# Moving early key transposes, summing early sketches in PSUM, moving the clears of later rows, and joining the last stores in a sketch-attention and top-2 expert kernel

## The chip, the cores and the metric

The kernel runs on one core of a Trainium2 chip. The metric is the device time in microseconds (us) of one execution; lower is better. The engines are TensorE (PE; PEld is its weight load), VectorE (DVE), ScalarE (ACT), GpSimd (POOL) and SyncE (SP). SP, ACT and POOL issue the DMA transfers here, and POOL also the indirect ones, which scatter rows to addresses held in a tile.

## The reference, cut to what matters

Everything is float32. Batch 4, 4 heads of 32 dimensions, 1088 tokens: 4352 tokens of width 128 in all. Eight experts with an inner width of 1024.

```python
def phi(x):                       # r = 8
    a = einsum('rd,bhsd->bhsr', S1, x)
    b = einsum('rd,bhsd->bhsr', S2, x)
    return einsum('bhsi,bhsj->bhsij', a, b).reshape(..., 64)
q_p, k_p = phi(q), phi(k)
kv  = einsum('bhsf,bhsd->bhfd', k_p, v)
z   = sum(k_p, axis=2)
x   = (q_p @ kv) / (q_p . z + 1e-6)          # per head, then heads side by side: 128 wide
logits = x @ w_gate
noisy  = logits + log1p(exp(x @ w_noise)) * noise
top2   = the two largest of noisy per token; weights = their softmax
out    = sum over the token's two experts of weight * (relu(x @ w1[e]) @ w2[e])
```

## The kernel before

**Order.** Nothing is issued in the order in which the program text stands. `plan.add` records a job with its engine or engines, an estimated cost, what it reads and writes, and a priority; `Plan.order` simulates the engines with these costs and, among the jobs that could start soonest, takes the one with the lowest priority number. Each engine and each queue then executes its jobs in that fixed order, so a job that waits holds up everything behind it on its engine. `idle` (line 1435 is its matmul) fills the planner's gaps on PE before 28 us with bf16 matmuls on a zero tile, `hp<-zb`, whose results nobody uses.

**The head (batch 0).** `sk` (L541) is the sketch matrix, split into a main part and a correction, `sk[:, 0]` and `sk[:, 1]`, 64 columns each. `turned` (L588, L590) transposes keys or queries on DVE into `kT` or `qT`. `features` multiplies up to four token tiles by all 128 columns of `sk` (L606) into one PSUM bank, copies the correction's half to `lo` (L322 is the copy helper), adds it to the main half into `ab` (L614) and forms the 64 products per head (`product`, L628) in `phk` or `phq`. `vaug` is the values with a column of ones, copied by ACT or POOL. L669 sums keys times values; two ACT copies make `kvT`; `fold` (L690) multiplies it by the gate weights; two copies make `kvw`, left and right columns of one tile. `queries` turns `phq` on PE (L717), copies it to `pT`, and L728 gives numerators, denominators and gate logits at once; `den` (L757) and `lg` (L747) follow on DVE.

**Routing.** `router` chooses the two experts of a tile's tokens and writes each weighted token row with its number to its expert's area in `xs`, one indirect scatter of 128 rows at a time (`xs<-xg,to`, L809; L808 is a short memset on POOL ahead of each as a spacer). One call of `router` is a wave; wave 0 is the first four tiles of batch 0, wave 1 the other five. Before a wave's rows are scattered, the rows it may reach must have been cleared: `clear` writes a pad tile of zeros over 128 rows of all experts, 516 KB each, issued by SP. Dependencies on `paces` put each scatter behind a chosen step of ACT or DVE.

**Expert blocks.** A block is one unit u: 128 or 256 rows of an expert. The first `DIRECT` = 4 units don't read `xs`: one-hots `o` on DVE (L1054), every fourth on ACT (L1047, L1050), gather the tokens by a matmul (`turn`, L1060). Units 4 to 7 are fetched by POOL and turned on PE (L1084); from 8 on SP fetches four pieces and DVE transposes them (L1096). `bT` is a unit's rows, transposed. L1108 multiplies them by `w1`, L1116 is the relu, L1123 multiplies by `w2` into `acc`; `y` is its copy, which POOL scatters to the token's place in `pairs`. For the first four units those places are in `first_at`, for the others in `ix`, fetched by SP.

**The end.** `sums` loads `pr` from `pairs`, adds a token's two results (L1179) and stores them. For the last batch the last two experts' results don't go through `pairs`: `to_tokens` adds them by one-hot matmuls (L1255) into `totals`, and `more` (L1186) adds those before the store, which ACT issues. There are three pieces: tiles 4 and 5, the 64 rows left over, tiles 6 and 7.

## Time and profile before

| | us |
|---|---|
| runs: median, lowest, highest | 346.61, 346.3, 347.8 |
| profiled execution, its own time | 347.08 |
| its span, from the first to the last instruction | 345.1 |
| busy: PE, POOL, DVE, ACT | 336.2, 232.1, 146.4, 136.4 |
| granted TensorE clock, mean over the span | 0.994 |
| first and second expert matmul of all blocks (L1108, L1123) | 147.3, 149.8 |

The rows of a timeline give the start, the length, the engine, the line, the operation, the tiles as output<-inputs and the count; consecutive instructions of one kind are drawn together. What stands in brackets is how long the engine had been idle and what ended that. A matmul in float32 appears as two records. A DMA row shows the issue on its queue, not the transfer.

### The profile page before, as it was taken

The page shows a single profiled execution, that of the slowest core. Times are in us where ns is not written, and L with a number is a line of the kernel's source. Part 1 is how long each engine was busy: PE and PEld are TensorE (multiplying, and loading weights), DVE is VectorE, ACT ScalarE, POOL GpSimd, SP SyncE. Part 2 cuts the span into 40 slices and gives each one's busy share as a digit, 9 for nine tenths or more (in the row PEclk, how much of TensorE's full clock was granted, in tenths as well). Part 3 has the DMA queues.
Part 4 walks back from the last instruction along what each step waited for, and adds up shares of the span by engine and source line. Part 5 has one row for each costly group of instructions (what it writes and reads, how often), then busy time and mean ns, then how long its engine had stood idle before and what let it go on. Part 6 is the DMA issues. An engine that isn't in the chain of part 4 may idle for free.

```text
span 345.1 us, 7493 instructions
## 1 busy us (share of the span) xinstructions
PE 336.2 (97%) x2585; PEld 313.9 (91%) x2586; DVE 146.4 (42%) x547; ACT 136.4 (40%) x305; POOL 232.1 (67%) x385
## 2 busy tenths in 40 slices
PE   8999999999999999999999999999999999999992
PEld 3859999999999999999999999999999999999992
DVE  5889794877636688555862000020102000112101
ACT  2357542543531445323334333433334333434430
POOL 8854868896899857898968889878334433354410
PEclk9999999999999999999999999999999999999997
DMA  7999839144571376511353213365125211114421
GB/s 217 327 346 268 288 63 356 60 116 114 139 221 39 62 187 133 138 40 39 74 74 71 54 43 54 69 184 120 37 36 185 67 32 27 29 32 166 147 77 39
DMA packets 68922, 41.17 MB, mean 119 GB/s; under 512 B 49877, under 2 KB 61078, under 8 KB 68880
## 3 DMA queue, kind: packets, MB, share of 16 engines
q1 hardware_dynamic: 63360, 30.93, 35.1%
q0 software_dynamic: 4704, 9.15, 8.2%
q10 hardware_dynamic: 816, 0.58, 0.6%
q8 instruction: 21, 0.34, 0.4%
q14 instruction: 21, 0.17, 0.2%
HBM read 24.18 MB, written 16.65 MB: 118 GB/s over the span
## 4 chain that ended last, share of the span: by engine, by line
PE 95%; DVE 2%; ACT 1%; issue 1%; POOL 0%; DVEq 0%; ACTq 0%; POOLq 0%
PE acc L1123 37%; PE hp L1108 37%; PE bank L606 5%; PE bank L728 4%; PE bank L669 4%; PE bank L717 2%; PE hp L1435 1%; PE acc L669 1%; PE bank L1255 1%; PE turn L1060 1%; PE bank L690 0%; ACT o L1050 0%; PE bank L937 0%; DVE lg L747 0%; ACT o L1047 0%
## 5 line engine op out<-in xcount | busy, mean ns | idle before, releaser
L1123 PEld LDWEIGHTS acc<-w2s,h 128*128 128x128 f32 x1152 | 145.8, 192 | 4.6
L1123 PE MATMUL acc<-w2s,h 128*128 128x128 f32 x1152 | 149.8, 275 | 0.0
L1108 PE MATMUL hp<-bT,w1s 128*128 128x128 f32 (+1 forms) x768 | 147.3, 328 | 0.2 <-ACT bT L322 0.2
L1116 ACT ACTIVATE h<-hp 128x512 f32<-128x512 f32 x144 | 86.0, 597 | 123.2 <-PE hp L1108 122.9
L1108 PEld LDWEIGHTS hp<-bT,w1s 128*128 128x128 f32 x768 | 111.6, 191 | 6.4 <-ACT h L1116 0.5
L809 POOL DMA_INDIRECT pairs<-y,ix x66 | 65.1, 986 | 66.1 <-ACT y L322 55.9
L809 POOL DMA_INDIRECT xs<-xg,to x72 | 73.0, 1014 | 19.2 <-issue 9.1
L808 POOL MEMSET zb<- 128x400 bf16 (+1 forms) x142 | 63.1, 444 | 0.2 <-PE hp L1435 0.2
L1096 DVE STREAM_TRANSPOSE bT<-xb 128x256 f32<-128x256 f32 (+1 forms) x40 | 15.6, 390 | 101.9 <-PE hp L1108 89.8
L322 ACT COPY y<-acc 128x128 f32<-128x128 f32 (+1 forms) x48 | 15.3, 320 | 28.1 <-PE acc L1123 27.6
L1179 DVE TENSOR_TENSOR o<-pr 128x512 f32<-128x512 f32 (+2 forms) x13 | 6.7, 525 | 36.1 <-DMA pr<-pairs 36.1
L728 PE MATMUL bank<-kvw,pT 128*128 128x98 f32 x144 | 18.2, 274 | 0.0
L728 PEld LDWEIGHTS bank<-kvw,pT 128*128 128x128 f32 x144 | 17.4, 192 | 0.6 <-DVE kvw L322 0.3
L669 PE MATMUL bank<-phk,vaug 128*128 128x128 f32 (+1 forms) x108 | 13.1, 277 | 0.0
L322 ACT COPY lo<-bank 128x256 f32<-128x256 f32 (+3 forms) x20 | 6.5, 328 | 16.5 <-PE bank L606 16.5
L322 ACT COPY pT<-bank 128x512 f32<-128x512 f32 (+1 forms) x16 | 8.8, 559 | 10.6 <-PE bank L717 9.1
L669 PEld LDWEIGHTS bank<-phk,vaug 128*128 128x128 f32 (+1 forms) x108 | 12.5, 191 | 0.4
L614 DVE TENSOR_TENSOR ab<-bank,lo 128x256 f32<-128x256 f32 (+3 forms) x20 | 7.2, 360 | 12.5 <-ACT lo L322 12.4
L628 DVE TENSOR_TENSOR phk<-ab 128x512 f32<-128x512 f32 (+1 forms) x20 | 12.2, 629 | 0.4
L628 DVE TENSOR_TENSOR phq<-ab 128x512 f32<-128x512 f32 (+1 forms) x20 | 11.8, 628 | 0.2
L991 DVE TENSOR_TENSOR xg<-x,g 128x512 f32<-128x512 f32 (+1 forms) x16 | 11.2, 750 | 0.0
L1435 PE MATMUL hp<-zb 128*128 128x512 bf16 x29 | 9.5, 463 | 1.6 <-DVE zb L439 1.3
(177 smaller groups left out, 243.7 us busy)
## 6 DMA issues: line engine op xcount, KB each, us to landing
xs<-pad SPq DMA_DIRECT2D x9, 516.0 KB
w1s<-in_moe_w_dram SPq DMA_DIRECT2D x8, 512.0 KB
w2s<-in_moe_w_dram SPq DMA_DIRECT2D x8, 512.0 KB
pr<-pairs SPq DMA_DIRECT2D x7, 512.0 KB
xb<-xs SPq DMA_DIRECT2D x96, 32.0 KB
kq<-in_k_dram SPq DMA_DIRECT2D x4, 544.0 KB
kq<-in_q_dram SPq DMA_DIRECT2D x4, 544.0 KB
vld<-in_v_dram SPq DMA_DIRECT2D x14, 128.0 KB
```

Of the source, the lines that this page charges most:

```text
L322: paces.append(A.copy(o, i) if e == "ACT" else V.tensor_copy(o, i))
L606: T.matmul(ps.t[rows, 2 * W * i:2 * W * i + 2 * W], lhsT=lhsT, rhs=sk[:].rearrange("p c h x -> p (c h x)"), start=True, stop=True)
L628: V.tensor_tensor(out=jobs[i][2].t[rows, jobs[i][1]:jobs[m - 1][1] + 1, :, :].rearrange("p c h (i j) -> p (c h) i j", i=R), in0=factors(i, ...
L669: T.matmul(kvp.t[:, P * a:P * a + P], lhsT=va.t[0:K, t, hs, :].rearrange("p h d -> p (h d)"), rhs=pk.t[0:K, t, hs, :].rearrange("p h f -> ...
L728: T.matmul(ps2.t[:, c0:c0 + 2 * YW], lhsT=pT.t[:, P * (2 * i + a):P * (2 * i + a) + P], rhs=kvw.t[:, a, :], start=True, stop=True)
L808: G.memset(zb[:, 0:FIRST_SPACER if kind == "first" else SPACER], 0.0)
L809: ins = G.indirect_dma_start(**kw)
L1096: add("DVE", vec(P * n), lambda _: V.transpose(bT.t[:, 0:P * n], flat()), r=[xb], w=[bT], prio=TOP + u)
L1108: T.matmul(hp.t[:, P * n * i:P * n * (i + 1)], lhsT=w1s[:, e, P * (js * g + i):P * (js * g + i + 1)], rhs=bT.t[:, 0:P * n], start=True, st ...
L1116: paces.append(A.activation(out=h.t[:], in_=hp.t[:], func=AF.Relu))
L1123: T.matmul(acc.t[:, D * c:D * c + D], lhsT=h.t[:, P * (n * i + c):P * (n * i + c + 1)], rhs=w2s[:, e, j, :], start=(j == 0 and c == 0), st ...
L1435: ins = T.matmul(warm()[:], lhsT=zb[:, 0:P], rhs=zb[:], start=True, stop=True)
```

## The change

- In the head, the first two tiles of keys are transposed before `sk` is made, and the other key transposes follow at once; `lo` is gone: the copy goes to `ab` and the add works in place.
- The early sketches, four tiles of queries of batch 0 and four of keys of batch 1, are each made by two matmuls of 64 columns that add up in PSUM, and ACT copies the result to `ab`.
- The two copies to `kvw` are one on ACT, one on DVE, and declared independent. The transposes of batch 1's keys follow them.
- On POOL the pad, the limits and the token numbers go behind the `vaug` copies, the limits in pieces, the last of them behind the first wave's choice of rows.
- The first unit's fourth one-hot is made by DVE as the others are.
- The clears of rows 256 to 511 go behind SP's four `ix` fetches; the planner treats two POOL jobs as behind the units' fetches. In the order that results, the clears of rows 0 to 255 stand behind the weights of expert 2 on SP, and POOL scatters the results of units 0 and 1 before the ten scatters of wave 1 (before: unit 0's alone).
- At the end the 64 rows come first and tiles 4 to 7 are read in two transfers and stored in one, two ACT issues for three. Tiles 0 to 3 of that batch are now read in two transfers too.

```diff
...
             for d in j.deps:
-                if d.engine == e and d.size is None and not d.far:
+                if d.engine == e and (d.size is None and not d.far or d in j.issued):
                     at = max(at, d.end)
...
     tag("qT", 1, [P, S])
-    tag("lo", 2, [P, 4, 2 * R * H])
-    tag("ab", 2, [P, 4 * H, 2, R])
+    tag("ab", 4, [P, 4 * H, 2, R])
     tag("kvT", 2, [P, 2, R * R])
...
-        add("POOL", cost, lambda e: emit(), r=r, w=w, prio=prio)
+        job = add("POOL", cost, lambda e: emit(), r=r, w=w, prio=prio)
+        if 11 < prio < 11.5:
+            behind_values.append(job)
+        if prio == 17:
+            behind_choices.append(job)
+
+    behind_values, behind_choices = [], []
...
-        pool_job(1.2, 13, pads, ["pad"])
+        pool_job(1.2, 11.45, pads, ["pad"])
...
-        pool_job(0.5, 14, lambda: limits(0, 1), [("limits", 0)], ["base"])
+        pool_job(0.5, 11.47, lambda: limits(0, 1), [("limits", 0)], ["base"])
...
                                channel_multiplier=2 * TN)
-        pool_job(2.4, 15, numbers, ["pid"])
-        pool_job(3.0, 16, lambda: limits(1, NW + 1), [("limits", 1)], ["base"])
+        pool_job(2.4, 11.4, numbers, ["pid"])
+        for w in range(1, NW + 1):
+            pool_job(0.5 if w < NW else 0.3, 16 if w < 4 else 17, lambda w=w: limits(w, w + 1), [("limits", 1)], ["base"])
         add("DVE", 0.3, lambda e: (V.tensor_copy(starts[:, 0, :], base[:]), V.memset(over[:], -1.0)),
...
-    def features(jobs, prio, after=(), first=None, early=None):
+    def features(jobs, prio, after=(), first=None, early=None, summed=False):
...
+                if summed:
+                    for c in range(2):
+                        T.matmul(ps.t[rows, W * i:W * i + W], lhsT=lhsT, rhs=sk[:, c, :, :].rearrange("p h x -> p (h x)"),
+                                 start=(c == 0), stop=(c == 1))
+                    continue
...
-        last = (add if early is None else plan.add)("PE", n * mm(128), emit, lat=0.15, r=["sk"] + [(xT, t) for xT, t, _ in jobs],
+        last = (add if early is None else plan.add)("PE", n * (2 * mm(64) if summed else mm(128)), emit, lat=0.15, r=["sk"] + [(xT, t) for xT, t, _ in jobs],
...
-        lo, ab = new("lo"), new("ab")
-        gone = [] if early is None else [onehot["pos"], onehot["gm"]]
+        ab = new("ab")
+        flat = lambda: ab.t[rows, 0:n * H, :, :].rearrange("p (i h) w r -> p i (h w r)", h=H)
...
-        add(EV, either(W * n), lambda e: copy(e, lo.t[rows, 0:n, :], x4()[:, :, 1, :]), r=[ps] + gone, w=[lo], prio=prio)
-        add("DVE", vec(W * n), lambda e: V.tensor_tensor(
-            out=ab.t[rows, 0:n * H, :, :].rearrange("p (i h) w r -> p i (h w r)", h=H),
-            in0=x4()[:, :, 0, :], in1=lo.t[rows, 0:n, :], op=ALU.add), r=[ps, lo], w=[ab], prio=prio if early is None else 12.95 if jobs[0][2] is kv_of[0][1] else 13.2)
+        if summed:
+            add("ACT", act(W * n), lambda e: copy(e, ab.t[rows, 0:n * H, :, :].rearrange("p x w r -> p (x w r)"), ps.t[rows, 0:W * n]),
+                r=[ps], w=[ab], prio=prio if early is None else 12, after=() if early is None else (onehot["sp"],))
+        else:
+            add(EV, either(W * n), lambda e: copy(e, flat(), x4()[:, :, 1, :]), r=[ps], w=[ab], prio=prio)
+            add("DVE", vec(W * n), lambda e: V.tensor_tensor(out=flat(), in0=x4()[:, :, 0, :], in1=flat(), op=ALU.add), r=[ps], w=[ab],
+                prio=prio)
...
-    behind_gates = []
+    behind_gates, folded_first = [], []
...
-            add(("ACT", "POOL") if head else "ACT", {"ACT": act(256), "POOL": 0.4} if head else act(256), lambda e, h=h: copy(e, va.t[:, 0:C, h, 0:DH], vld.t[:, h, 0:C, :]),
-                r=["ones_v"] + [(vld, l) for l in range(4)], w=[(va, h)], prio=prio + 2.2, after=hold)
+            value = add(("ACT", "POOL") if head else "ACT", {"ACT": act(256), "POOL": 0.45} if head else act(256),
+                        lambda e, h=h: copy(e, va.t[:, 0:C, h, 0:DH], vld.t[:, h, 0:C, :]),
+                        r=["ones_v"] + [(vld, l) for l in range(4)], w=[(va, h)], prio=prio + (2.05 if head else 2.2), after=hold)
+            if head:
+                for job in behind_values:
+                    job.deps.add(value)
...
-                turned(kT, kld, c0, c1, 22, True)
-                features([(kT, t, pk) for t in range(c0, c1)], prio + i + 1, after, 21.5, early)
+                turned(kT, kld, c0, c1, 22, True).deps.update(folded_first)
+                features([(kT, t, pk) for t in range(c0, c1)], prio + i + 1, after, 21.5, early, True)
...
-            freed.append(turned(kT, kld, c0, c1, prio + i))
+            freed.append(turned(kT, kld, c0, c1, (-51, 0.5, 0.9)[i] if head else prio + i))
...
-        freed.append(turned(kT, kld, 8, 9, prio + 1))
+        freed.append(turned(kT, kld, 8, 9, prio + (1.9 if head else 1)))
...
-            add(EV, either(98), lambda e, l=l: copy(
-                e, kvw.t[64 * l:64 * l + 64, :, YW * l:YW * l + YW],
-                ps.t[64 * l:64 * l + 64, 0:2 * YW].rearrange("p (a y) -> p a y", a=2)),
-                r=[ps, "kvw0"], w=[(kvw, l)], prio=prio + 3)
+            def half(e, l=l):
+                ins = copy(e, kvw.t[64 * l:64 * l + 64, :, YW * l:YW * l + YW],
+                           ps.t[64 * l:64 * l + 64, 0:2 * YW].rearrange("p (a y) -> p a y", a=2))
+                if head:
+                    apart(ins, "kvw")
+                    wrote(ins, "kvw")
+            done = add(("ACT", "DVE")[l] if head else EV, 0.25 if head else either(98), half, r=[ps, "kvw0"], w=[(kvw, l)], prio=prio + 3)
+            if head:
+                folded_first.append(done)
...
-                features([(qT, t, pq) for t in range(4, 8)], prio + 26, (), prio + 11, early)
+                features([(qT, t, pq) for t in range(4, 8)], prio + 26, (), prio + 11, early, True)
...
         actf(0.25, lambda: A.activation(out=t3("u"), in_=t3("u"), func=AF.Exp), ["u"], ["u"])
-        actf(0.25, lambda: A.activation(out=t3("sp"), in_=t3("u"), func=AF.Ln, bias=1.0), ["u"], ["sp"])
+        soft = actf(0.25, lambda: A.activation(out=t3("sp"), in_=t3("u"), func=AF.Ln, bias=1.0), ["u"], ["sp"])
+        onehot.setdefault("sp", soft)
         def noise_of():
...
-        add("POOL", 0.25, lambda e: G.tensor_scalar(out=g1(), in0=g2(), scalar1=1.0, scalar2=1e-9, op0=ALU.add, op1=ALU.add),
-            r=[(B_["g"], 1)], w=[(B_["g"], 0)], prio=prio - 0.5)
+        sums_of[w] = add("POOL", 0.25, lambda e: G.tensor_scalar(out=g1(), in0=g2(), scalar1=1.0, scalar2=1e-9, op0=ALU.add, op1=ALU.add),
+                         r=[(B_["g"], 1)], w=[(B_["g"], 0)], prio=prio - 0.5)
         dve(0.2, lambda: V.reciprocal(g1(), g1()), [(B_["g"], 0)], [(B_["g"], 0)], -0.5)
...
         indexed = dve(0.2 + 2 * vec(16 * n), index, ["first", "row"], ["f2", "at", "to"], late)
+        while behind_choices:
+            behind_choices.pop().deps.add(indexed)
         xg, to = B_["xg"], B_["to"]
...
-                if c == 3:
-
-                    add("ACT", act(P), lambda e_, c=c: A.activation(
+                if c == 3 and u:
+
+                    add("ACT", 0.45, lambda e_, c=c: A.activation(
...
-                    add("ACT", act(P), lambda e_, c=c: A.activation(
+                    add("ACT", 0.45, lambda e_, c=c: A.activation(
...
                             there, [xb], -10 + u, size=66e3 * n, issue=0.55, done=done)
+                sums_of[1].deps.add(fetch)
+                sums_of[1].issued.add(fetch)
                 for job in held[DIRECT]:
...
-            dma("SP", lambda: ix.t[:, 0:n].unsqueeze(2), lambda: rows[:, D:XW].rearrange("(c p) x -> p c x", p=P),
-                there, [ix], -10 + u + (0.5 if u < QUICK else 0), size=0, issue=0.5, done=done)
+            numbers_in = dma("SP", lambda: ix.t[:, 0:n].unsqueeze(2), lambda: rows[:, D:XW].rearrange("(c p) x -> p c x", p=P),
+                             there, [ix], -10 + u + (0.5 if u < QUICK else 0), size=0, issue=0.5, done=done)
+            if u == QUICK - 1:
+                for job in behind_numbers:
+                    job.deps.add(numbers_in)
+                    job.issued.add(numbers_in)
...
-            dma("SP", lambda t=t, rows=rows, cs=cs: t.t[rows, cs, :, :].rearrange("p c k d -> p (c k d)"), lambda src=src: src,
-                [key for w in range(last + 1) for key in results[w]], [(t, c0)], prio, size=1024.0 * c * rows.stop, done=done)
-            add("DVE", vec(P * c), lambda e, t=t, o=o, rows=rows, cs=cs: V.tensor_tensor(
-                out=o.t[rows, cs, :], in0=t.t[rows, cs, 0, :], in1=t.t[rows, cs, 1, :], op=ALU.add),
-                r=[(t, c0)], w=[(o, c0)], prio=prio)
+            n = 2 if b == B - 1 and c == 4 else c
+            for d in range(0, c, n):
+                ds = slice(c0 + d, c0 + d + n)
+                dma("SP", lambda t=t, rows=rows, ds=ds: t.t[rows, ds, :, :].rearrange("p c k d -> p (c k d)"),
+                    lambda src=src, d=d, n=n: src[..., 2 * D * d:2 * D * (d + n)],
+                    [key for w in range(last + 1) for key in results[w]], [(t, ds.start)], prio, size=1024.0 * n * rows.stop, done=done)
+                add("DVE", vec(P * n), lambda e, t=t, o=o, rows=rows, ds=ds: V.tensor_tensor(
+                    out=o.t[rows, ds, :], in0=t.t[rows, ds, 0, :], in1=t.t[rows, ds, 1, :], op=ALU.add),
+                    r=[(t, ds.start)], w=[(o, ds.start)], prio=prio)
...
-                tot = totals[at]
-
-                def more(e, o=o, tot=tot, rows=rows, cs=cs):
-                    V.tensor_tensor(out=o.t[rows, cs, :], in0=o.t[rows, cs, :],
-                                    in1=tot.t[rows, 0:P * (cs.stop - cs.start)].rearrange("p (c d) -> p c d", d=D), op=ALU.add)
-                add("DVE", vec(P * c), more, r=[tot, (o, c0)], w=[(o, c0)], prio=prio)
-            dma(queue, lambda dst=dst: dst, lambda o=o, rows=rows, cs=cs: o.t[rows, cs, :].rearrange("p c d -> p (c d)"), [(o, c0)],
+                for k in (range(1, 3) if c > 1 else (0,)):
+                    def more(e, o=o, rows=rows, k=k):
+                        ks, tot = slice(2 * k - 2, 2 * k) if k else slice(0, 1), totals[k]
+                        V.tensor_tensor(out=o.t[rows, ks, :], in0=o.t[rows, ks, :],
+                                        in1=tot.t[rows, 0:P * (ks.stop - ks.start)].rearrange("p (c d) -> p c d", d=D), op=ALU.add)
+                    add("DVE", vec(P * min(c, 2)), more, r=[totals[k]], w=[(o, 2 * k - 2 if k else 0)], prio=prio)
+            dma(queue, lambda dst=dst: dst, lambda o=o, rows=rows, cs=cs: o.t[rows, cs, :].rearrange("p c d -> p (c d)"), [(o, c0 + d) for d in range(0, c, n)],
...
-        for k, cols in enumerate(((0, 1), (4,), (2, 3))):
+        for k, cols in enumerate(((4,), (0, 1), (2, 3))):
...
-                for i, c in enumerate(cols):
+                for c in cols:
...
-                    T.matmul(totals[k].t[0:M, D * i:D * i + D], lhsT=oh.t[:, P * c:P * c + M], rhs=y.t[:, 0:D],
-                             start=(e == E - LAST and i == 0), stop=(e == E - 1), skip_group_check=True)
+                    T.matmul(totals[k].t[0:M, D * (c % 2):D * (c % 2) + D], lhsT=oh.t[:, P * c:P * c + M], rhs=y.t[:, 0:D],
+                             start=(e == E - LAST and c % 2 == 0), stop=(e == E - 1), skip_group_check=True)
...
         job.deps.update(freed)
-    for r in (2 * P, 3 * P):
-        clear(r, 52)
+    behind_numbers = [clear(r, 52) for r in (2 * P, 3 * P)]
     load_v(1, 49.5)
...
             sums(B - 1, part_of(B - 1, [(0, 4)]), w, 901)
-    pieces = part_of(B - 1, [(4, 2), (6, 2)], True)
-    sums(B - 1, [pieces[0], pieces[2], pieces[1]], NW, 902, ("ACT",))
+    pieces = part_of(B - 1, [(4, 4)], True)
+    sums(B - 1, [pieces[1], pieces[0]], NW, 902, ("ACT",))
...
```

## The prediction

> **What bounds the kernel now.** I read the page's busy shares and its chain first, then three stretches in order of time: the head (to the first expert matmul), the packed middle, the end.
>
> ```profile
> PE 336.2 (97%) x2585; PEld 313.9 (91%) x2586; DVE 146.4 (42%) x547; ACT 136.4 (40%) x305; POOL 232.1 (67%) x385
> ...
> PE 95%; DVE 2%; ACT 1%; issue 1%; POOL 0%; DVEq 0%; ACTq 0%; POOLq 0%
> ```
>
> TensorE is the chain. The same profile cut into three windows says where it is full:
>
> ```profile
> 0.00:27.47 27.47, 25.09 (x157) 16.68 (x159) 20.45 (x82) 11.19 (x40) 18.98 (x81) 1.00 0.95 298
> 27.47:337.20 309.73, 309.43 (x2418) 296.03 (x2418) 124.80 (x463) 125.02 (x266) 213.13 (x304) 1.00 0.41 105
> 337.20:345.10 7.90, 1.72 (x10) 1.23 (x10) 1.16 (x4) 0.24 (x1) 0.00 (x0) 0.72 0.14 43
> ```
>
> The columns are length, then busy time of PE, its weight loads, DVE, ACT, POOL; then clock, DMA share, GB/s. In the middle PE is busy 309.43 of 309.73 us, so what comes earlier at 27.47 ends as much earlier, if PE meets no new wait. In the head PE looks busy too, but much of that is `hp<-zb` matmuls of line 1435 that only keep it running; the head is a chain through all engines. Its links that the change touches, in the timeline (start, length, what; in brackets idle time and releaser):
>
> ```profile
> 6.15 0.29 DVE L541 TENSOR_TENSOR sk<-bank,own 128x128 f32<-128x128 f32 x1 [0.60 <-PE bank L536]
> 6.36 1.03 DVE L590 STREAM_TRANSPOSE kT<-kq 128x256 f32<-128x256 f32 x2
> 6.85 2.11 PE L606 MATMUL bank<-sk,kT 128*128 128x128 f32 x14 [0.15 <-DVE kT L590]
> ...
> 16.32 0.23 ACT L322 COPY kvw<-bank 64x98 f32<-64x98 f32 x1
> 16.58 0.26 DVE L322 COPY kvw<-bank 64x98 f32<-64x98 f32 x1 [0.98 <-ACT kvw L322]
> 16.90 1.86 PEld L728 LDWEIGHTS bank<-kvw,pT 128*128 128x128 f32 x16 [0.28 <-DVE kvw L322]
> ...
> 26.90 0.35 ACT L322 COPY lo<-acc 128x256 f32<-128x256 f32 x1
> 27.15 0.27 ACT L322 COPY bT<-turn 128x128 f32<-128x128 f32 x1
> 27.28 0.42 DVE L614 TENSOR_TENSOR ab<-acc,lo 128x256 f32<-128x256 f32 x1 [0.53 <-ACT lo L322]
> 27.47 1.60 PE L1108 MATMUL hp<-bT,w1s 128*128 128x128 f32 x12 [0.24 <-ACT bT L322]
> ```
>
> DVE idles 0.60 us before `sk`; the second `kvw` copy waits for the first, though they write different columns; and `lo` stands in ACT's queue ahead of the `bT` that the first expert matmul needs. The end:
>
> ```profile
> 338.70 3.04 ACTq L338 DMA_DIRECT2D out_dram<-o  x3
> 339.25 0.42 DVE L1186 TENSOR_TENSOR o<-o,bank 128x256 f32<-128x256 f32 x1 [0.36 <-PE bank L1255]
> ```
>
> The last sum is ready at 339.67, but the third store is issued only at 341.04: the second store's issue lasts from 339.45 to 340.95. Landings read from the trace's events: 341.72, 342.5, 343.285. The closing waits end at 345.06, 1.77 later.
>
> **The change, step by step.** *Keys ahead of the sketch.* The first `kT` transpose (0.44 for 128x256) moves into DVE's gap 5.55 to 6.15. Keys landed at 5.61, so it ends about 6.1 and `sk` stays at 6.15. The first sketch then waits for `sk` alone (6.44 + 0.06) and starts at 6.50 instead of 6.85. `kvT` sums (L669) start at 9.94 now, behind all key sketches (from 9.42, 0.68 long; their wait and the two dummies ahead of them go as the transposes come earlier). POOL's two `vaug` copies become the other bound: the pad memset and iota (7.33 to 8.52) leave, two limit pairs (4 at about 0.2 net, from the rows 17.25 to 18.43) come in their place, so the copies end near 9.2 instead of 9.51. Between DVE's -0.35 and -0.6 from PE and POOL I take -0.45 for this step.
>
> *The copies of `kvw` side by side.* The second ends at 16.58 instead of 16.84. But PE has two turns (L717) from 16.20 to 16.86 there, and the slot after them is free near 16.75. So -0.15, from 0 to -0.28 (the row's idle time). At `den` that makes -0.6.
>
> *First expert's one-hots.* The fourth moves from ACT (L1047 0.40, L1050 0.49) to DVE, whose one-hots start every 0.256 from 25.13: it ends at 25.898 + 0.34 = 26.24, against ACT's 26.17; the fourth turn starts at 26.485 in PE's order and isn't delayed. With `lo` gone from its place, `bT` can start when the turns end (26.87 + 0.04 = 26.91) instead of 27.15: -0.24. `row` isn't behind the 0.42 of `ab` any more, so the first scatters gain some 0.6.
>
> *Summed sketches.* Sixteen records of 128 columns (0.11 apart, 1.8 us) become 32 of 64. The nearest row for few columns is L690's 8 records of 49 columns in 0.54, which makes 32 x 0.06 = 1.9 us. But these load only 64 weight columns. The Trainium skill ("TensorE: Matmul & The Clock Gate", LDWEIGHTS) speaks against the change here: a load costs its columns / 1.2 ns, 107 ns for 128, whatever is streamed, so 32 x 0.107 = 3.4 us, nearly double. PE's loads here are indeed about 0.116 apart (16 in 1.86 at L728), so I take 3.4. It is covered: this stands among the dummies of 18.8 to 24.6, and the planner books 0.205 for each narrow matmul and sends fewer dummies. Uncovered it would cost 1.6. The `ab` copies (2 x 0.37) come on ACT behind `sp`, where it waits for `g` until 23.36: nothing. Two DVE adds of 0.42 go: no bound after 28.
>
> *Queues.* SP: clears of rows 0 and P go behind the weights of expert 2 and their pad is now filled at about 15; they need to land before the first scatter (29.88 now, some 14 us on), and the keys of batch 1 no longer stand behind the first clear: landed 15.94, now about 15, wanted at 16.6 by a DVE transpose that now precedes `den`. If late by x, `den` is late by x. Limits and `pid` on POOL end earlier than the 19.79 they do now; `a` is wanted at 19.7: nothing. Clears of rows 2P and 3P are issued after the four `ix` (43.91 to 45.67), so land near 49 to 50, beside the fetches of units 4 to 7 on POOL (44.41 to 46.63); unit 4's was landed at 46.66, ahead of them. Wave 1's scatters wait for these clears but start at 52.74 now.
>
> *One more scatter ahead of wave 1.* POOL sends unit 1's result first: one 1.575-us step. It starts when the first wave-1 scatter did, 52.74 - 0.84, so the ten scatters run from 53.5, 0.7 later (0.4 at best). Behind the last are unit 8's fetches:
>
> ```profile
> 52.74 1.10 POOL L809 DMA_INDIRECT xs<-xg,to  x1 [0.45 <-ACT h L1116]
> ...
> 69.63 1.76 SPq L338 DMA_DIRECT2D xb<-xs  x4
> ```
> ```profile
> 74.61 0.31 DVE L1096 STREAM_TRANSPOSE bT<-xb 128x128 f32<-128x128 f32 x1
> ```
>
> They landed at 72.62 and were transposed at 74.61: 2.0 us of cover. The need comes 0.84 earlier and the landing 0.7 later, so 0.4 of cover is left and PE doesn't wait. Without cover it costs 1 us for each us.
>
> *The end.* The 64-row piece is summed and stored first (issue near 338.3), the two halves go in one 256-KB store, issued at 339.69. By the rows a 128-KB store lands 2.25 (third) to 3.02 (first) after its issue; 128 KB more took 0.5 of packets. So 342.45 to 343.2. The skill ("SBUF — State Buffer", the DMA setup-cost knee) has 2 us + bytes / 436 GB/s, an estimate of 2.6 and 342.3. If the long 1.50-us issue falls on the second store again, it is about 343.2. I take 342.55, nearer to the third store's row, since the queue is running by then: -0.7, from 0 to -1.0.
>
> **Sum.** Head -0.45 - 0.15 - 0.24 = -0.84 (bounds -0.6 to -1.1); middle 0 (the same matmuls in another order); end -0.7. Span 345.1 - 1.54 = 343.56; the profiled execution 347.08 becomes 345.5. The median of the runs, 346.61, is 0.47 below that one: **345.1**. A measurement of this kernel tells from no change about 0.5%, 1.73 us: the line to "faster" is 344.88, that to "slower" 348.34.
>
> **Rivals.** *Unit 8 too late (slower).* Place: the first matmul of unit 8. If the clears of 2P and 3P land after 53.5, or POOL's scatters with their waits on block steps run over 1.6 each, the fetch slips; it decides from 0.4 us of slip. The clears are 1 MB at some 0.33 MB per us beside fetches: for a start 3.7 us late (PE stalled 3.3 + DVE's router work queued behind that transpose) they must land near 57. Then 346.6 - 1.5 + 3.3 or more: 348.4 and up. For it: 0.4 is little, and DVE is in order. Against: over 3 us of margin before 53.5.
> *The change doesn't shorten the path.* `kT` delays `sk` (keys 0.1 late), `vaug` still bounds L669, the store's long issue stays: -0.4, 346.2. For it: keys landed only 0.06 after the gap opens.
> *All bounds on the good side.* Head -1.1, end -1.0, and the 0.4-us stall at 107.6 gone: 344.1. For it: the rows leave room at each step.
>
> **Chances.** Forecast (344.4 to 345.7) 0.52, all good 0.16, no gain 0.12, unit 8 or another late transfer 0.20. Faster by over 0.5%: 0.16 and half of the forecast's, 0.42; within: 0.26 + 0.12 = 0.38; slower: 0.20. The range 344.0 to 348.3 leaves the fast tail and the worst stalls out.
>
> **What would show it.** L606 at 6.5; `kvw` copies together and L728 at 16.3 or so (-0.6); `bT` right behind the turns and the first expert matmul at 26.6; no idle time of PE near 72 to 76; last sum at 338.8, one 256-KB issue of 0.7, landed 341.7. Wrong if `sk` moves later, if PE waits at unit 8, or if the issue takes 1.5 us.

## The result: 0.3% slower, with the head and the end shorter and the middle longer

The changed kernel takes 347.83 us (median of 14 runs, 347.26 to 348.8) against 346.74 for the kernel before on the same chip: a ratio of 1.003, 95% interval 1.0018 to 1.0042. The forecast was 345.1, 0.5% faster. A loss of 0.3% lies inside the 0.5% band, but the interval excludes no change, and the sign of the forecast was wrong.

The profiled execution took 348.23 us, 0.4 above the median, with a span of 346.5; the one of the kernel before was 0.5 above its own, so the two can be compared. First its busy shares and its chain, from the page:

```profile
PE 336.8 (97%) x2594; PEld 315.5 (91%) x2594; DVE 146.6 (42%) x548; ACT 135.6 (39%) x302; POOL 233.1 (67%) x385
...
PE 79%; DVE 5%; DMA 5%; POOL 4%; SPq 3%; issue 2%; ACT 0%; DVEq 0%; POOLq 0%
```

The busy time of PE has hardly moved (336.2 before). The chain has: PE was 95% of it, now it is 79%, and DVE, DMA, POOL and SP hold 17%. In the traced execution something other than PE decides for some tens of microseconds. The same three windows as before, cut at the first expert matmul and 0.3 us before the last one-hot sums (length, busy time of PE, weight loads, DVE, ACT, POOL; clock, DMA share, GB/s):

```profile
0.00:26.35 26.35, 24.61 (x167) 17.82 (x167) 20.76 (x84) 10.74 (x39) 18.31 (x81) 1.00 0.96 296
26.35:339.15 312.80, 310.63 (x2419) 296.51 (x2418) 124.69 (x462) 124.57 (x264) 214.84 (x304) 1.00 0.41 106
339.15:346.50 7.35, 1.52 (x10) 1.16 (x10) 1.13 (x4) 0.25 (x1) 0.00 (x0) 0.83 0.14 46
```

| window | before | after | difference | forecast |
|---|---|---|---|---|
| head, to the first expert matmul | 27.47 | 26.35 | -1.12 | -0.84 |
| middle | 309.73 | 312.80 | +3.07 | 0 |
| end | 7.90 | 7.35 | -0.55 | -0.70 |

The whole surprise is in the middle. It holds the same number of PE records, 2419 against 2418, and it lost 3.07 us. The two longest waits of PE between 26 and 337 us (engine, tile and line, what it waited for and from which engine; then us in total, how often, the longest):

```profile
PE bank L619 <- DVE kT L598: 1.1, 1, 1.1
PE turn L1114 <- DMA xb<-xs: 0.5, 1, 0.5
```

Before, neither was there. Measured by the spacing of PE's records, four pauses are new: 0.65 at 46.75 (the turn of unit 4, fetched by POOL), 0.27 at 78.88 (an expert matmul that needs a `bT` from DVE), 1.21 at 88.56 (batch 2's key sketch) and 0.31 at 109.23. That is 2.44 of 3.07. The rest is small pieces, which I didn't assign. After 115 us PE is full in both kernels.

The timeline shows how the largest pause comes about: SP's fetches, POOL's scatter, DVE's transposes and PE's sketch in the changed kernel, then the same transposes and the sketch in the kernel before:

```profile
43.56 2.59 SPq L339 DMA_DIRECT2D ix<-xs  x4
46.19 1.19 SPq L339 DMA_DIRECT2D xs<-pad  x2
54.86 0.96 POOL L834 DMA_INDIRECT xs<-xg,to  x1 [0.17 <-issue]
71.24 1.78 SPq L339 DMA_DIRECT2D xb<-xs  x4
78.42 0.31 DVE L1126 STREAM_TRANSPOSE bT<-xb 128x128 f32<-128x128 f32 x1 [0.90 <-DMA xb<-xs]
82.75 0.31 DVE L1126 STREAM_TRANSPOSE bT<-xb 128x128 f32<-128x128 f32 x1 [2.55 <-DMA xb<-xs]
87.81 1.29 DVE L598 STREAM_TRANSPOSE kT<-kq 128x512 f32<-128x512 f32 x2
88.56 2.05 PE L619 MATMUL bank<-sk,kT 128*128 128x128 f32 x16 [1.05 <-DVE kT L598]
```
```profile
80.83 0.31 DVE L1096 STREAM_TRANSPOSE bT<-xb 128x128 f32<-128x128 f32 x1 [0.86 <-DMA xb<-xs]
85.89 1.30 DVE L590 STREAM_TRANSPOSE kT<-kq 128x512 f32<-128x512 f32 x2
87.68 1.95 PE L606 MATMUL bank<-sk,kT 128*128 128x128 f32 x16
```

The first scatter of wave 1 starts at 54.86 (before 52.74) and unit 8's fetch at 71.24 (before 69.63). DVE executes in order, so its transposes wait for units 8 to 10, the last for 2.55 us (before, only that last one waited, 0.86). Everything behind them on DVE moves, the transposes of batch 2's keys to 87.81 (before 85.89), and PE, which was ready for them at 87.35, stands still.

The delay also grows on SP itself. In the changed kernel, then in the kernel before, the issues that follow unit 8's fetch:

```profile
73.07 1.82 SPq L339 DMA_DIRECT2D ix<-xs  x1
74.99 1.80 SPq L339 DMA_DIRECT2D xb<-xs  x4
```
```profile
71.44 0.43 SPq L338 DMA_DIRECT2D ix<-xs  x1
71.97 1.81 SPq L338 DMA_DIRECT2D xb<-xs  x4
```

One `ix` issue takes 1.82 us instead of 0.43, so unit 9's fetch is 3.0 later than before and unit 10's, from 77.40, 2.5. What was under way beside it is shown with runs e8 and e10.

### The profile page after: what moved, and what is told of

The parts are those of the page before. It is cut to its first block, busy times and chain, and to the rows that moved or that the text cites. A ratio compares the mean times of both kernels' runs of the same rounds, so it can differ in the third digit from the quotient of the medians.

```text
span 346.5 us, 7503 instructions
## 1 busy us (share of the span) xinstructions
PE 336.8 (97%) x2594; PEld 315.5 (91%) x2594; DVE 146.6 (42%) x548; ACT 135.6 (39%) x302; POOL 233.1 (67%) x385
## 4 chain that ended last, share of the span: by engine, by line
PE 79%; DVE 5%; DMA 5%; POOL 4%; SPq 3%; issue 2%; ACT 0%; DVEq 0%; POOLq 0%
PE acc L1157 33%; PE hp L1142 31%; PE bank L753 4%; SPq L339 3%; POOL xs L834 3%; DMA xb<-xs 3%; PE bank L619 3%; PE bank L689 2%; DMA xs<-xg,to 2%; PE bank L742 2%; PE hp L1472 1%; PE acc L689 1%; POOL zb L833 1%; DVE phq L644 1%; DVE xg L1019 1%
## 5 line engine op out<-in xcount | busy, mean ns | idle before, releaser
L834 POOL DMA_INDIRECT xs<-xg,to x72 | 75.4, 1047 | 16.9 <-issue 9.9
L322 ACT COPY ab<-bank 128x256 f32<-128x256 f32 (+3 forms) x20 | 6.5, 327 | 18.2 <-PE bank L619 18.2
L322 ACT COPY pT<-bank 128x512 f32<-128x512 f32 (+1 forms) x18 | 9.7, 550 | 9.9 <-PE bank L742 9.1
L742 PE MATMUL bank<-ident,phq 128*128 128x128 f32 x72 | 10.9, 278 | 0.0
L619 PE MATMUL bank<-sk,kT 128*128 128x128 f32 (+1 forms) x64 | 9.0, 283 | 1.2 <-DVE kT L598 1.1
```

The source lines that it names most:

```text
L322: paces.append(A.copy(o, i) if e == "ACT" else V.tensor_copy(o, i))
L619: T.matmul(ps.t[rows, 2 * W * i:2 * W * i + 2 * W], lhsT=lhsT, rhs=sk[:].rearrange("p c h x -> p (c h x)"), start=True, stop=True)
L742: T.transpose(ps.t[:, c0:c0 + P], pq.t[:, t + i, 2 * a:2 * a + 2, :].rearrange("p h f -> p (h f)"), ident[:])
L834: ins = G.indirect_dma_start(**kw)
```

## The experiments

All ratios are against the kernel before, run beside each kernel on the same chip. "Lead" is how much earlier than before a given expert matmul starts. "Order" is the order of PE's instructions, the dummies left out.

A trace shows one execution, and what a run is worth is taken from the medians. The kernel e3 below has before's order up to the end, and its first expert matmul starts here:

```profile
27.17 2.05 PE L1108 MATMUL hp<-bT,w1s 128*128 128x128 f32 x16 [0.23 <-ACT bT L322]
```

In the trace of the kernel before it is at 27.47, so a lead of 0.3 us between two traces says nothing by itself. The traced executions of e1 and e11 were 0.4 and 0.5 us faster than their medians, those of the kernel before and the changed kernel 0.5 and 0.4 slower. The device time is also longer than the span, by 1.7 to 1.8 us in the changed kernel, e1, e2, e4 and e11 and by 2.0 to 2.3 in the others; what fills that time is not known.

### Do the late clears make the loss? e1 and e2

```diff
 e1_clears_early, against the changed kernel
-    behind_numbers = [clear(r, 52) for r in (2 * P, 3 * P)]
+    behind_numbers = []
+    for r in (2 * P, 3 * P):
+        clear(r, 52)
```

> The changed kernel with one part undone: the clears of rows 256 to 511 go back ahead of the four ix fetches on SP, and as the planner then finds wave 1's scatters ready, no result scatter stands ahead of them. Theory (late clears delay first_at and the results of units 0 and 1, these delay wave 1's ten scatters, these the fetches of units 8 to 10, on which DVE and then PE wait): first_at landed near 49.3 instead of 50.7, first wave-1 scatter near 51.5 instead of 54.86, unit 8 fetched near 68.5 instead of 71.24, no wait of DVE on xb over 1 us and no 1.2-us wait of PE at the kT sketch; PE keeps its 1.1 of the head, the end its 0.55: span 343.4, about 1.6 below before. Rival (PE's new order makes the waits by itself): PE's order is nearly the changed kernel's, the waits of 0.27 and 1.21 stay, span 346 or more.

Measured: 1.0018 (1.0007 to 1.0029), 347.67 us, span 345.5. The clears go at 31.40, the first wave-1 scatter starts at 50.32, unit 8's fetch at 67.41, and of DVE's waits for units 8 to 10 one of 1.05 is left. Both expectations missed: the theory had a span of 343.4, the rival 346 or more. In the medians the run is 0.67 us above before, the changed kernel 1.09, and their intervals overlap. PE waits elsewhere instead:

```profile
PE acc L1157 <- ACT h L1150: 0.7, 1, 0.7
PE turn L1114 <- DMA xb<-xs: 0.4, 1, 0.4
PE hp L1142 <- issue: 0.3, 1, 0.3
```

So the clears are at most a part. The order changed in places too, which spoils the comparison. The next kernel keeps the clears late and hides from the planner that wave 1 waits for them, which gives exactly e1's order on every engine but SP:

```diff
 e2_clears_late_no_result_ahead, against the changed kernel
-                pair = add("POOL", ROWS + 0.3, emit, r=[...] + [("clear", r) for r in range(0, REACH[w], P)],
+                pair = add("POOL", ROWS + 0.3, emit, r=[...] + [("clear", r) for r in range(0, REACH[w] if w != 1 else 2 * P, P)],
```

> The changed kernel with the clears left behind the ix fetches, but the planner not told that wave 1 waits for them: PE's and POOL's orders are those of the run with early clears, only SP's place of the clears differs; the scatters still wait for the landing on the chip. Theory 1 (both matter: the late clears hold the first wave-1 scatter until they land near 52.9, the result scatters added 1.6 each): first wave-1 scatter near 53.2, unit 8 fetched near 69.6, PE waits little there: 0.5 to 1 us above the run with early clears. Theory 2 (only the result scatters ahead matter): as the run with early clears within 0.3 us. Theory 3 (only the clears matter): as the changed kernel within 0.3 us.

Measured: 1.017 (1.0143 to 1.0198), 352.63 us (five runs), 5.0 more than e1; the expectation had at most 1 us. The first wave-1 scatter, with its idle time, and PE's largest pause:

```profile
54.17 1.12 POOL L834 DMA_INDIRECT xs<-xg,to  x1 [5.08 <-DVE ab L631]
```
```profile
85.16 0.22 PE L960 MATMUL bank<-mk,earlier 128*128 128x72 bf16 x1 [3.35 <-DVE mk L953]
```

POOL stands for 5.08 us in front of that scatter, which came at 50.32 in e1. The second late clear landed at 53.26; the row names what came last, DVE's `ab` at 54.12. Unit 8's fetch is issued at 71.51, and the router's one-hots `mk` on DVE, behind the waiting transposes, hold PE for 3.35 us. After so long a wait PE also ran at half its clock for a while (length, busy time of PE, then the other engines; the clock is the third number from the right):

```profile
85.16:88.57 3.41, 3.41 (x24) 3.41 (x24) 2.46 (x8) 0.27 (x1) 1.34 (x3) 0.50 0.30 50
88.57:92.00 3.43, 3.43 (x33) 3.43 (x33) 3.36 (x10) 1.46 (x3) 2.60 (x4) 1.00 0.80 214
```

In these 3.41 us its matmuls come 0.21 apart instead of 0.11, which adds about 1.5 us to the wait. With one and the same order the late clears cost 5 us. That is the rival "unit 8 too late" in full size, at another place than it named. But the changed kernel's own fetch is nearly as late, 71.24, and there PE loses far less. The lateness is one part of the price; what PE has planned for those microseconds is the other.

### The end and the head by themselves: e3, e4, e5

`e3_before_with_new_end` is the kernel before with the change's end alone (the 64 rows first, tiles 4 to 7 in one store):

```diff
...
-    pieces = part_of(B - 1, [(4, 2), (6, 2)], True)
-    sums(B - 1, [pieces[0], pieces[2], pieces[1]], NW, 902, ("ACT",))
+    pieces = part_of(B - 1, [(4, 4)], True)
+    sums(B - 1, [pieces[1], pieces[0]], NW, 902, ("ACT",))
...
```

> The kernel before with the new end alone (64 rows first, four tiles read in two, stored in one); all other orders are unchanged. Theory: the end gains 0.55 by itself as in the changed kernel's trace: 346.2 against 346.75, ratio 0.9984. Rival (the changed kernel's shorter end comes from elsewhere, or the closing waits end with something other than the store): ratio 1.000.

Measured: 0.9984 (0.9974 to 0.9994), 346.43 us against 347.0. The end is worth 0.57, as expected (0.55).

`e4_clears_early_old_end` is e1 with the old end.

> The run with early clears with the old end put back: what the head is worth alone. Theory: PE's lead of 1.1 us at the first expert matmul lasts to the end: 1.1 below before, ratio 0.997, and 0.55 above the run with early clears. Rival (the lead is taken back later by waits on transfers whatever the clears do): ratio 0.999 to 1.002.

Measured: 1.0038 (1.0026 to 1.0049), 348.39 us, span 347.3. The expectation missed. Outside the end its order is e1's, and so are its pauses: 1.13 at unit 4's turn, 0.99 for a relu on ACT, 0.75 for DVE at 123.70, where e1 has 0.56, 0.83 and 0.42. PE leads by 1.15 at the first expert matmul and is 2.20 behind at the last, with no late clears at all. The 0.72 us to e1's median are about what e3 gives for the end.

`e5_before_keys_kvw_end` has the keys ahead of the sketch, the two `kvw` copies side by side and the new end in the kernel before; the order of PE behind the head stays:

```diff
...
-            freed.append(turned(kT, kld, c0, c1, prio + i))
+            freed.append(turned(kT, kld, c0, c1, (-51, 0.5, 0.9)[i] if head else prio + i))
...
-            add(EV, either(98), lambda e, l=l: copy(
+            add(("ACT", "DVE")[l] if head else EV, 0.25 if head else either(98), half, r=[ps, "kvw0"], w=[(kvw, l)], prio=prio + 3)
...
```

> The kernel before with three parts of the change: keys transposed ahead of the sketch, the two kvw copies side by side, the new end. The order of work on every engine and queue after the first 18 us stays that of before. Theory (re-planned order: what lost the gain is that the planner lays out everything after 28 us anew, with waits its estimates don't see): PE's lead of some 0.5 us lasts, with the end's 0.55: about 1.0 below before, ratio 0.997. Rival (transfers set PE's pace after the head, so a lead is lost at unit 4 or 8 whatever the order): only the end's 0.55, ratio 0.9984.

Measured: 0.9982 (0.9973 to 0.9991), 346.07 us, span 344.6. That is the gain of the end and no more, as the rival had it: the lead of 0.37, hardly more than e3's 0.30 without any edit in the head, is lost in one place, a pause of 0.77 at unit 4's turn, and from there to the end PE runs 0.43 *later* than before. The keys' step is there in full (the keys-times-values sums start at 9.27, in the changed kernel at 9.30), but the `kvw` copies start at 16.15, not 15.77; what the rest of the change does in between was not tried by itself.

### One edit, two orders: e6 and e7

`e6_before_dve_onehot` is the kernel before with nothing but the first unit's fourth one-hot on DVE. `e7_before_dve_onehot_same_order` is the same, with 0.2 us more in the planner's estimate for the first unit's `bT` copy, a number that issues no instruction but brings the order back: in the trace PE, DVE, POOL and SP have exactly before's:

```diff
 e6, against the kernel before
-                if c == 3:
+                if c == 3 and u:
...
 e7: this, and
-            add(EV, either(P * n), lambda en: copy(en, bT.t[:, 0:P * n], turn.t[:, 0:P * n]), r=[turn], w=[bT], prio=TOP + u)
+            add(EV, either(P * n) if u else {"ACT": act(P) + 0.2, "DVE": vec(P) + 0.2}, lambda en: copy(en, bT.t[:, 0:P * n], turn.t[:, 0:P * n]), r=[turn], w=[bT], prio=TOP + u)
```

> The kernel before with one part of the change alone: the first unit's fourth one-hot on DVE. Nothing else is edited, but the planner then orders PE, DVE and ACT anew from about 27 us on. Re-planned order: PE leads by 0.2 to 0.3 at the first expert matmul and then meets new waits of over 0.5 us in sum: ratio 1.000 to 1.006. Rival (the waits of the changed kernel come from its transfers alone): the lead stays or is lost at unit 4, ratio 0.999 to 1.000, no new wait of PE over 0.3 us.

> As the run before it, but the planner is told that the first unit's bT copy takes 0.2 us more than it estimates; with that its order after 27 us is that of the kernel before (but for one dummy matmul and the places of a lo copy and a vaug copy on ACT). Re-planned order: no new waits, ratio 0.999 to 1.000 and 0.5 us or more below the run with the new order. Rival: as that run within 0.3 us.

Measured: e6 1.0031 (1.0017 to 1.0046), 347.85 us; e7 0.9993 (0.9978 to 1.0007), 346.63 us. The intervals don't meet: for one and the same work, 1.2 us by the order alone. Both ratios are as expected, but e7 was to have no new wait and has one. PE's waits in e6, then in e7:

```profile
PE bank L717 <- ACT pT L322: 0.7, 1, 0.7
```
```profile
PE turn L1084 <- DMA ix<-xs: 0.8, 1, 0.8
```

e6 starts its first expert matmul 0.53 ahead and ends 0.58 behind: a new pause of 0.84 at 105.12, one of some 0.25 at 60.24, and small ones. It has neither late clears nor an extra scatter, and is as slow as the changed kernel. e7's lead of 0.58 goes in one place again, a pause of 0.96 at unit 4's turn. The row names `ix`, but the turn reads the fetched rows `xb`, and the last piece of that fetch landed at 48.22, 0.04 ahead of it.

### What holds unit 4: e8 and e10

`e8_best_of_both` is e5 with e7's two edits: the head edits of both, the new end, and before's order.

> Keys ahead of the sketch, kvw side by side, the DVE one-hot with the 0.2 us, the new end; the clears, the summed sketches and POOL's order stay as before, and the order after 27 us is that of before. Re-planned order: leads of 0.5 and 0.2 and the end's 0.55 add up: about 1.2 below before, ratio 0.9965, the fastest of all. Rival: 0.9984, the end alone.

Measured: 0.9985 (0.9976 to 0.9994), 346.18 us, span 344.4: again the rival, the end alone. The lead of 0.57 becomes 0.22 behind, at unit 4's turn:

```profile
48.08 0.33 PE L1088 MATMUL turn<-ident,xb 128*128 128x128 f32 x1 [0.62 <-DMA xb<-xs]
```

The landing events show each fetch in sixteen pieces. Of unit 4's in e8 the first is in at 46.20, the last at 48.03, and the fetches issued behind it trail by as much (unit 5's from 46.82 to 48.45); in the kernel before it was 46.28 to 46.66. A view of the DMA traffic from 45 to 46 us in e8 shows what else was under way, besides the fetch:

```profile
q8 instruction: 1, 0.02, 5.8%
```

One packet of 0.02 MB of PE's own program, about 1 us long on one of the sixteen DMA engines. It starts at 45.93 in e8, 45.92 in e5 and 45.66 in e7, and the last piece lands at 48.0 to 48.2 in all three; in the kernel before it starts at 47.13, behind the fetch, which is in at 46.66. The Trainium skill ("Runtime: NRT & Kernel Launch", Instruction fetch mechanics) has engines fetch their instructions in blocks of 16 KiB, 256 instructions, through a queue of their own, the cost mostly hidden. The packet's size, 16,384 bytes, agrees, and so does the cost to PE: in the kernel before thirteen such packets start between 115 and 335 us, where PE is busy 220.00 of 220.00. The cost to a transfer beside it is another matter. If the packet delays the fetch beside it, twenty tiny matmuls at the start (40 more instructions) bring the next block's packet earlier and the wait at unit 4 goes:

```diff
 e10_best_with_20_tiny_matmuls, against e8
+            if a == 0:
+                for i in range(20):
+                    T.matmul(warm()[:, 0:1], lhsT=zb[:, 0:P], rhs=zb[:, 0:1], start=True, stop=True)
```

> The kernel of run e8 with 20 matmuls of one column ahead of the others at the start, where PE waits for the first inputs: 40 more instructions in PE's program, no other difference in order. In the runs where unit 4's rows landed 1.3 to 1.5 us after their first pieces, a packet of the instruction queue, 1 us long, lay at 45.1 to 45.9, within the fetch; in those where they landed within 0.4 us it lay at 47 or later. Theory (that packet holds up one of the fetch's 16 engines, and its time goes with PE's place in its program): the packet moves 2 to 3 us earlier, to about 43.5, unit 4's rows land near 46.7, PE's wait of 0.76 there goes, and the time falls by 0.5 to 0.8 below run e8: ratio 0.996 to 0.997. Rival (the late pieces have another cause, such as the scatters or the clears): the wait stays at 0.6 to 0.9, ratio as e8, 0.9985.

Measured: 0.9982 (0.9969 to 0.9994), 346.19 us, span 344.1, the time of e8. The mechanism did what was expected: the packet went at 43.79, unit 4 was in at 46.38, and PE's turn does not wait:

```profile
47.78 0.31 PE L1088 MATMUL turn<-ident,xb 128*128 128x128 f32 x1
```

The expected gain did not come, since the lead went too: the first expert matmul starts at 27.48, where e8 had it at 27.00. The start of the two traces shows why. PE's transposes for `sk` stand behind the dummies; first e10, then e8:

```profile
1.27 0.69 PE L1444 MATMUL hp<-zb 128*128 128x1 bf16 x20 [1.27 <-DVE zb L440]
5.75 0.28 PE L537 MATMUL bank<-ident,s 16*128 16x16 f32 x1
```
```profile
5.22 0.28 PE L537 MATMUL bank<-ident,s 16*128 16x16 f32 x1
```

The twenty matmuls push the nine dummies behind them from 1.27 to 1.82, these the transposes, and `sk` comes at 6.69 instead of 6.27. So e10 supports the packet as the cause of the late piece, and leaves its worth in time open: the means of moving it took back the lead.

The same packets bear on SP's slow `ix` issue. In the changed kernel one was under way from 73.20 for 1.29 us, just at that issue; in the kernel before it came at 77.72, beside a load of `vld` whose issue took 1.71 us. In all thirteen traces, every issue of SP of over 0.8 us between 66 and 90 us overlaps such a packet. That is a coincidence in time, which no run here tested, and one trace does not show whether the changed kernel's packet stands there in each execution.

### All of the change but the late clears, in another order: e9 and e11

`e9_all_but_clears_old_order_late` is the changed kernel without the late clears and the two planner dependencies, and with 0.3 us more in the same estimate as in e7. From about 60 us its PE order is before's; ahead of that it puts two sketches before unit 4's turn.

```diff
 against the changed kernel
-                sums_of[1].deps.add(fetch)
-                sums_of[1].issued.add(fetch)
...
-            add(EV, either(P * n), lambda en: copy(en, bT.t[:, 0:P * n], turn.t[:, 0:P * n]), r=[turn], w=[bT], prio=TOP + u)
+            add(EV, either(P * n) if u else {"ACT": act(P) + 0.3, "DVE": vec(P) + 0.3}, lambda en: copy(en, bT.t[:, 0:P * n], turn.t[:, 0:P * n]), r=[turn], w=[bT], prio=TOP + u)
...
-    behind_numbers = [clear(r, 52) for r in (2 * P, 3 * P)]
+    behind_numbers = []
+    for r in (2 * P, 3 * P):
+        clear(r, 52)
```

> The changed kernel without the move of the clears of rows 256 to 511 and without the two POOL jobs set behind the fetches, and with 0.3 us added to the planner's estimate of the first bT copy: PE's order is then that of the kernel before from about 60 us on; between 28 and 60 us it still differs, and unit 4's turns come later on PE than before. Theory (what the change gains is kept when the planned order holds no new waits): PE leads by 1.1 at the first expert matmul, loses at most 0.4 up to 60 us, nothing after; with the end's 0.55 the span is 343.5 to 343.9, ratio 0.995 to 0.9965. Rival (the summed sketches, the shared ab buffers or POOL's new order cost time of their own): new waits of PE after 60 us, ratio 0.998 or more.

Measured: 0.998 (0.9969 to 0.999), 345.68 us, span 343.4. It beats both kernels. The result lies between the expectations: there are no new waits after 60 us and the span is even a little below the theory's, but the ratio is the rival's. The span is also close to the 343.56 that the prediction had for the change, but that was reckoned from a traced execution 0.5 us slower than the median; in the medians e9 gains 0.84 us, where 1.5 was forecast. The lead is 0.73 at the first expert matmul and 0.76 from 70 us on to the last block. Some 0.4 of the head was given away by the estimate itself, since the planner filled the longer copy with two dummies:

```profile
26.30 0.60 PE L1472 MATMUL hp<-zb 128*128 128x512 bf16 x2
26.74 1.95 PE L1140 MATMUL hp<-bT,w1s 128*128 128x128 f32 x16
```

`bT` started at 26.04 there, as in the changed kernel (26.03), whose expert matmul follows at 26.35. Unit 4 is in at 46.94; PE turns it after two sketches and doesn't wait:

```profile
46.83 1.47 PE L619 MATMUL bank<-sk,qT 128*64 128x128 f32 x10
48.13 0.27 PE L1112 MATMUL turn<-ident,xb 128*128 128x128 f32 x1
```

`e11_after_old_order_clears_late` is the changed kernel with that estimate alone. Its order on PE is near e9's, but its clears are late and unit 1's result goes ahead of wave 1.

> The changed kernel with one number of the planner's altered (0.3 us more for the estimate of the first unit's bT copy), so that TensorE's order after 60 us is nearly that of e9_all_but_clears_old_order_late. Against e9 it differs in what the change does with the clears of rows 256 to 511: they stand behind the four ix on SP, and unit 1's result goes ahead of the ten scatters of wave 1 on POOL. Theory one (the order alone makes the loss of the middle, the late clears are hidden in a good order): lead of 0.7 to 0.8 kept to the end, span 343.4 to 343.9, ratio 0.998. Theory two (the late clears cost by themselves, through unit 8's fetch and the DVE transposes behind it): the first wave-1 scatter near 54.9 and unit 8's fetch near 71.2 as in the changed kernel, DVE waits for xb of units 8 to 10, PE loses 0.7 to 2 between 72 and 115; span 344.3 to 345.7, ratio 1.000 to 1.004. I hold the second likelier, with about half of the changed kernel's 3.1 us of loss in the middle.

Measured: 0.9996 (0.998 to 1.0012), 346.63 us, span 344.4: between the two expectations, and the one held likelier fell where it counts. The first wave-1 scatter (54.20) and unit 8's fetch (70.54) are late nearly as in the changed kernel, DVE waits, and PE between 72 and 115 us loses nothing:

```profile
81.42 0.31 DVE L1126 STREAM_TRANSPOSE bT<-xb 128x128 f32<-128x128 f32 x1 [1.96 <-DMA xb<-xs]
86.47 1.30 DVE L598 STREAM_TRANSPOSE kT<-kq 128x512 f32<-128x512 f32 x2
87.63 1.95 PE L619 MATMUL bank<-sk,kT 128*128 128x128 f32 x16
```

The sketch comes up at 87.63, when its first transpose has just been made: the cover is used up, but not overdrawn. But the supply is not quite the changed kernel's: its `ix` issue took 0.43, unit 10's fetch started at 75.81 instead of 77.40, and the transpose at 81.42 is 1.3 earlier than there. What e11 lost against e9, 0.66 on PE, is ahead of 43.28 (0.49, a late relu on ACT) and of 47.91; the first lies ahead of the clears, issued at 46.76. The remaining third of a microsecond is in the end.

So a fetch of unit 8 at 70.5 to 71.5 costs PE nothing in e11, 1.2 to 1.5 us in the changed kernel, and over 3 us in e2: it depends on how late units 9 and 10 are then, and on what the order has PE do at 80 to 89 us. The four kernels side by side, in medians:

| | clears | order of PE | against before, us | interval of the ratio |
|---|---|---|---|---|
| changed kernel | late | its own | +1.09 | 1.0018 to 1.0042 |
| e1 | early | nearly its own | +0.67 | 1.0007 to 1.0029 |
| e11 | late | nearly e9's | -0.21 | 0.998 to 1.0012 |
| e9 | early | before's from about 60 us on | -0.84 | 0.9969 to 0.999 |

## Why the prediction was wrong, step by step

**Sum, the term "middle 0 (the same matmuls in another order)", failed.** It measured +3.07. The claim rested on PE's 309.43 busy of 309.73 before: true for that order, in which each input came in time, and nothing said that another order keeps this. e6 against e7 shows 1.2 us for the order alone, with one identical edit. In the changed kernel the other order takes back 1.3 us with the clears late (e11) and 1.5 with them early (e9 against e1); the early clears take back 0.4 and 0.6, which the intervals do not tell from nothing. This division holds for these orders only: in e2's, which is e1's, the late clears cost 5.0. And it is not clean, since e11's supply of units 9 and 10 was also less late.

**Queues and one more scatter ahead of wave 1: the mechanism was right, its size was not.** The slip of unit 8's fetch was put at 0.7; it measured 1.61. The term that was too small is the start of the result scatters. The fetch of `first_at` landed at 50.69 (before 49.59) although it was issued 0.35 earlier, so they began at 51.49 instead of 50.57. Where a clear is issued ahead of that fetch, it took 4.4 and 4.6 us (changed kernel, e2); where none is, 2.3 to 3.0 (before, e1, e9, e11). The clears themselves landed at 50.58 and 52.84, not 49 to 50, but POOL was busy with the result scatters until 54.24, so that was not the limit. The first wave-1 scatter came at 54.86, the forecast had 53.5.

**The 2.0 us of cover were read at unit 8 alone.** Its transpose had them. Unit 10's had none: in the kernel before it already waited 0.86 us for its fetch (the row at 80.83), so each later fetch pushed DVE from there on. Unforeseen was also the `ix` issue of 1.82 us.

**The rival "Unit 8 too late" came true at a smaller price and in a place beside the one it named.** It put the stall at unit 8's first matmul. There PE doesn't wait (nothing near 72 to 76, as the forecast said). It pays 13 us later, through DVE's order, which the rival had in a half sentence. Its 3.3 us are seen only in e2.

**Head: right, within the scatter of single traces.** *Keys ahead of the sketch:* forecast -0.45. The keys-times-values sums start at 9.30 against 9.94, but in e3, e6 and e7, with before's head up to there, at 9.65 to 9.74; between the means of four traces without and eight with this step (e10 left out) lie 0.49. *The `kvw` copies:* forecast -0.6 in all up to here; L728 starts at 16.18 against 16.90, and 0.57 lie between the means. *First expert's one-hots:* forecast -0.84 in all; the two traces with before's head and the four with the changed kernel's (this one, e1, e2, e4) are 0.94 apart at the first expert matmul.

```profile
5.90 0.45 DVE L598 STREAM_TRANSPOSE kT<-kq 128x256 f32<-128x256 f32 x1 [0.40 <-DMA kq<-in_k_dram]
6.27 0.25 DVE L549 TENSOR_TENSOR sk<-bank,own 128x128 f32<-128x128 f32 x1
6.58 2.22 PE L619 MATMUL bank<-sk,kT 128*128 128x128 f32 x16
...
15.77 0.26 DVE L322 COPY kvw<-bank 64x98 f32<-64x98 f32 x1 [0.71 <-PE bank L710]
15.78 0.23 ACT L322 COPY kvw<-bank 64x98 f32<-64x98 f32 x1
...
26.03 0.27 ACT L322 COPY bT<-turn 128x128 f32<-128x128 f32 x1 [0.71 <-PE turn L1088]
```

The rival that `kT` delays `sk` came true in part: `sk` starts at 6.14 to 6.43 in the eight traces with the transpose ahead of it, at 5.87 to 6.15 in the four without, and the first sketch gains 0.11 between the means, not 0.35. The two `kvw` copies start within 0.01 of each other, and `bT` follows the turns directly.

**Summed sketches: right, and by the Trainium skill's rule rather than by the row.** The 32 records of 64 columns, by their tile (shortest, median and longest in ns; first and last start):

```profile
L616 PE MATMUL acc<-sk,qT x16: 247/275/275, 18.0 to 19.7; 128*128 128x64 f32 x16
L616 PE MATMUL acc<-sk,kT x16: 275/275/275, 19.8 to 21.4; 128*128 128x64 f32 x16
```

They fill 18.01 to 21.55, 3.54 us; the rule of "TensorE: Matmul & The Clock Gate" (LDWEIGHTS) gave 3.4, the row of narrow matmuls 1.9. Dummies follow directly (from 21.55), so this cost nothing.

**The end: right, 0.15 too large.** Forecast -0.7, measured -0.55 in the span, and -0.57 in e3's medians. The two stores and the sums ahead of the second:

```profile
340.24 1.80 ACTq L339 DMA_DIRECT2D out_dram<-o  x2
340.57 0.87 DVE L1224 TENSOR_TENSOR o<-o,bank 128x256 f32<-128x256 f32 x2 [0.36 <-PE bank L1293]
```

The last sum is ready at 341.44 and the store has landed at 344.35, 2.91 later, which is the forecast's interval (338.8 to 341.7).

**What the working lacked** is the second bound of the head. Unit 4's landing was noted (46.66, ahead of the clears) but not weighed against a PE that comes 0.84 earlier. In before's order PE asked for it 1.2 us after it landed. A lead of 0.84 still fitted into that, but in e5, e7 and e8 the landing itself moved to 48.0 to 48.2 and took 0.8 to 1.0. In the changed kernel it stayed at 46.71, and PE lost 0.65 there because it came for the rows earlier still, at 46.10. First the kernel before, then the changed kernel:

```profile
47.88 0.31 PE L1084 MATMUL turn<-ident,xb 128*128 128x128 f32 x1
```
```profile
46.75 0.33 PE L1114 MATMUL turn<-ident,xb 128*128 128x128 f32 x1 [0.51 <-DMA xb<-xs]
```

## What to carry to other kernels

An edit in front of a planner changes every decision behind it, so compare the planned orders of all engines first, and measure such an edit once with the downstream order held fixed, which here took one number in one estimate; then see what that number itself moves (two dummies in e9). A lead on the bounding engine lasts only to the next input whose supply doesn't move with it: list those inputs with their landing times and subtract the lead from each margin, the later ones of a row of fetches too. An engine that executes in order hands a late input on to everything behind it, so look for the price of a late fetch at the next work of that engine, not at the fetch.

## What the runs showed of the hardware

- A packet of a program's own instructions occupies one of the sixteen DMA engines for 0.9 to 1.5 us and can hold back one sixteenth of a 64-KB fetch: with the packet starting at 44.8 to 45.9 (e1, e2, e4, e5, e7, e8, e11) unit 4 was in at 47.5 to 48.3; with it at 43.8 to 44.3 (changed kernel, e9, e10) or past 47 (before, e3, e6), at 46.3 to 46.9. e10 moved the packet on purpose and the late piece went, which supports it; that both were on the same DMA engine isn't shown.
- After PE had stood still for 3.35 us in e2, its granted clock was 0.50 for 3.41 us (85.16 to 88.57). Waits of up to 1.05 us (changed kernel, at 88.56) left it at 1.00.
- The third scatter of wave 0 took 2.97 us on POOL in the changed kernel, e1, e2, e4, e9 and e11, and 1.36 before; its cause is open. It used up most of the 1.55 us by which the first scatter came earlier (28.33 against 29.88): unit 4's fetch was issued only 0.35 earlier.
